# A spectral-mixing and expert kernel: all x of batch 0 loaded ahead of the weights, float64 conversions emitted behind the first FFT stage, GpSimd's tensor operations given to VectorE

## The chip, the core and the metric

The kernel runs on one core of a Trainium2 chip. The metric is device time in microseconds (us) from one launch. The engines are TensorE (PE; its weight loads are PEld), VectorE (DVE), ScalarE (ACT), GpSimd (POOL) and SyncE (SP), which here only issues DMAs. Each engine works through its own list of instructions in order, and waits on semaphores for the others.

## The reference

Three layers follow each other on x of 4 batches x 3072 positions x 256 channels.

```python
X = np.fft.fft(np.fft.fft(x, axis=1), axis=2).real          # 1: mixing by FFT
xp = concatenate([zeros, X[:, :-1]], axis=1)                # 2: channel mix with the position before
k = np.maximum((mu_k * X + (1 - mu_k) * xp) @ w_k, 0)       #    w_k 256 x 1024, w_r 256 x 256, w_v 1024 x 256: float64
y = sigmoid((mu_r * X + (1 - mu_r) * xp) @ w_r) * (k * k @ w_v)
e = argmax(y @ w_gate)                                      # 3: one of 8 experts for each token
out = softmax(y @ w_gate)[e] * sigmoid((y @ w_output_gate)[e]) * (relu(y @ w1[e]) @ w2[e])
```

## The kernel before

**Stage A, the FFT.** The 3072 positions are split into 24 x 128. In the first stage (`a_steps`, lines 264 to 290, called A1 here) seven x tiles of a batch, each of two windows of 512 columns (the last of one), are multiplied with a 120 x 120 matrix of cosines and sines (`fc`); ScalarE copies the products out of PSUM, and they are stored to a DRAM buffer, `scr`. An x tile is loaded by one DMA (`load_x`, line 243) whose pattern has 5 groups of 24 rows of 4 KB. For batch 0 the products overwrite the x tile, the matrices are float32 in one product, and GpSimd's queue issues the stores; for later batches x is split into a high and a low float32r half (ScalarE copies, another engine subtracts) and three products are added, and ScalarE's queue issues the stores. The second stage (A2, lines 291 to 375) reads `scr` back in six groups (`raw`, with tables `tb`), forms sum and difference `s` and `t` of the channel halves, folds them by symmetry (about eight short VectorE operations a group), and multiplies twice; the results go into `xt`, one batch in SBUF.

**Stage B, the channel mix.** `b_block` works on blocks of 512 tokens, six a batch, in the order `BLOCKS`. `mix_steps` forms the two mixed inputs and splits them into high and low halves. Eight steps f each take six matmuls with w_k, a relu and a square on ScalarE and VectorE with a split, and, two steps later, six matmuls with w_v. Between these steps `step(f)` advances A1 and A2 of the coming work and the mixing of the next block; `tail_steps` does the gate logits and writes rows and lists of tokens for stage C, the experts.

**The weights.** w_k, w_r and w_v come as float64 and are turned into two float32r halves by `convert` (line 195), nine units of 128 x 512: one DMA (`both`, 512 KB), on ScalarE an absolute value and a copy (the high half), on VectorE two integer operations (lines 213, 216) and three with two inputs (214, 215, 217), and on GpSimd two subtract-and-add operations for the low half (220, 221). Units 0 to 4 are w_r and w_k; they take buffers of the later `kh`, `kl`, `qh`, `ql` and `t1` tiles, and the fifth waits for the buffer of the first. Units 5 to 8 are w_v.

**GpSimd's tensor operations** are 34: two for each of nine conversions, `s` and `t` of four groups of batch 0 (lines 316, 317), and eight splits of x of batch 1 (line 281).

**What sets the order.** The program is written with a tile framework. Instructions are emitted by the Python code in the order in which it runs; a planner then walks through a modelled execution when the kernel is built, and at each moment gives each engine the first emitted of the instructions that are ready in its model. The result is one fixed list for each engine. SyncE issues nearly all loads. `load_later` keeps a load behind the second load of `raw` once that has been emitted. The start is emitted in the order of lines 531 to 541: seven x loads with the loads and conversions of w_r and w_k between them, constants, A1 of batch 0 (32 steps of its generator), the matrices `mc`, two groups of A2 (10 steps), small constants, the mixing of the first block, the clearing of the lists, and all four conversions of w_v. Block 0 follows.

Of the kernel before, what the change touches and what calls it, by code (L numbers as in the profile page):

```python
# [10 lines left out]
F32 = mybir.dt.float32  # L11
# [5 lines left out]
ALU = mybir.AluOpType  # L17
# [76 lines left out]
def moe_kernel(ctx: ExitStack, tc: tile.TileContext, x, mu_k, mu_r, wk2, wv2, wr2, wg, wo, w1, w2,  # L94
# [7 lines left out]
    def tt(o, a, b, op, eng=None):  # L102
        return (eng or DVE).tensor_tensor(out=o, in0=a, in1=b, op=op)  # L103
# [15 lines left out]
    a1 = sa.enter_context(tc.tile_pool(name="a1", bufs=2, side="right"))  # L119
    a2 = sa.enter_context(tc.tile_pool(name="a2", bufs=2, side="right"))  # L120

# [1 line left out]
    ident = const.tile([128, 128], F32, name="ident")  # L123
    acc = const.tile([128, 2, 5, E], BF16, name="acc")
    early = const.tile([128, 1, E], F32, name="early")
# [27 lines left out]
    def load_later(o, i):  # L153
        follow(SP.dma_start(o, i), raws[1:2], mybir.DependencyClass.NoSync, "the first groups come first")

    def split(h, l, src, eng=None):
        return act_copy(h, src), tt(l, src, h.bitcast(F32), ALU.subtract, eng)

    def setup_first():
        split(fh, fl, fc)  # L160
        POOL.memset(f0, 0.0)
        POOL.memset(xt[:, :, 0, 0:1], 0.0)
        POOL.memset(acc[:, 0, 0, :], 0.0)
        POOL.memset(early, 0.0)
        ACT.activation(out=ready, in_=early[:, 0], func=ACTF.Sigmoid)
        make_identity(nc, ident)
# [8 lines left out]
    def setup_second():  # L175
        mc = bp.tile([128, 2, 2, 128], F32, name="mc", tag="y", bufs=1)
        SP.dma_start(mc, c_m.rearrange("p (a b c) -> p a b c", a=2, b=2))
        split(mh, ml, mc)

    def setup_third():  # L180
        load_later(sm, c_s[:, 0:8 * E].rearrange("p (a b c) -> p a b c", a=2, b=4))
        load_later(cid, c_id.rearrange("p (a b c) -> p a b c", b=4, c=2))
        rt = bp.tile([128, 2, 128], F32, name="rt", tag="y", bufs=1)
        load_later(rt, c_r.rearrange("p (a b) -> p a b", a=2))
        act_copy(ones_tri, rt)
        wgf = bp.tile([128, 2, 2, E], F32, name="wgf", tag="lg", bufs=1)
        for j, m in enumerate((mu_k, mu_r)):
            load_later(mu[:, j], m.rearrange("(p c) -> p c", c=2))
        for j, w in enumerate((wg, wo)):
            load_later(wgf[:, :, j], w.rearrange("(c p) e -> p c e", p=128))  # L190
        DVE.tensor_scalar(omu, mu, -1.0, 1.0, ALU.mult, ALU.add)
        wgv = wgf.rearrange("p c j e -> p c (j e)")
        split(wgs[:, :, 0:16], wgs[:, :, 16:32], wgv)

    def convert(h, l, src):
        n = next(units)
        if n < 5:
            both = bp.tile([128, 1024], I32, name="both", tag="kh" if n % 2 else "kl")
            a = bp.tile([128, 512], I32, name="ca", tag="qh", bufs=3)
            b = bp.tile([128, 512], I32, name="cb", tag="ql", bufs=3)  # L200
            g = bp.tile([128, 512], F32, name="cg", tag="t1")
        else:
            if n == 5:
                spare.extend(bp.tile([128, 2, 512], d, name="spare", tag=t, bufs=1)
                             for d, t in ((I32, "yh"), (I32, "yl"), (F32, "y")))
            both = bp.tile([128, 1024], I32, name="both", tag="row")
            a, b, g = (t[:, n % 2] for t in spare)
        load_later(both.rearrange("p (a b) -> p a b", a=src.shape[1]), src.bitcast(I32))
        lo, hi = both[:, 0:1024:2], both[:, 1:1024:2]
        w = bp.tile([128, 512], F32, name="cw", tag="mx")  # L210
        af, bf = a.bitcast(F32), b.bitcast(F32)
        ACT.activation(out=g, in_=hi.bitcast(F32), func=ACTF.Abs)
        DVE.tensor_scalar(a, hi, 3, 0x3FFFFFF8, ALU.logical_shift_left, ALU.bitwise_and)
        stt(a, hi, -0x40000000, a, ALU.bitwise_and, ALU.bitwise_or)
        stt(af, g, SMALLEST, af, ALU.is_ge, ALU.mult)
        DVE.tensor_scalar(b, a, -0x800000, None, ALU.bitwise_and)
        stt(w, lo.bitcast(U32), 2.0 ** -52, bf, ALU.mult, ALU.mult)
        flat = lambda t: t.rearrange("p a b -> p (a b)")
        act_copy(flat(h), af)
        tt(af, af, flat(h).bitcast(F32), ALU.subtract, POOL)  # L220
        tt(flat(l), af, w, ALU.add, POOL)

    units, spare = iter(range(9)), []

    def convert_k(c, q):
        cols = slice(q * 512, q * 512 + 512)
# [7 lines left out]
        convert(wvh[:, 2 * q:2 * q + 2], wvl[:, 2 * q:2 * q + 2],  # L234
                wv2.rearrange("(c p) f -> p c f", p=128)[:, 2 * q:2 * q + 2])

# [1 line left out]
    def mm3(ps, ah, al, bh, bl, start=True, stop=True):  # L238
        PE.matmul(ps, ah, bh, start=start, stop=False)  # L239
        PE.matmul(ps, al, bh, start=False, stop=False)  # L240
# [8 lines left out]

    def load_first_x():  # L250
        places = [(a1, "xs", 3)] * 3 + [(bp, "yh", 1), (bp, "yl", 1), (bp, "rs", 1), (bp, "row", 2)]
        for i, (pool, tag, bufs) in enumerate(places):
            first_x.append(pool.tile([120, 2, 512], F32, tag=tag, name="xs", bufs=bufs))
            load_x(first_x[i], 0, i)
            if i == 0:
                SP.dma_start(fc, c_f)
            if i >= 3:
                early_units[i - 3]()
        early_units[4]()

    def a_steps(b):
        scr = dram.tile([24, 130, 256], F32, name="scr", tag="scr", bufs=2)
        sv = scr.rearrange("s (g m) d -> g s m d", g=5)
        for w in range(13):
            if w % 2 == 0:
                if b == 0:
                    e = xs = first_x[w // 2]
                else:
                    xs = a1.tile([120, 2, 512], F32, tag="xs", name="xs", bufs=3)
                    i = load_x(xs, b, w // 2)  # L270
                    follow(i, raws[2:3], mybir.DependencyClass.NoSync, "the first groups come first")
                    e = a1.tile([120, 2, 512], F32, tag="e", name="e", bufs=2)
            k_ = 120 if w < 12 else 96
            ps = pm.tile([120, 512], F32, tag="m", name="ps1")
            if b == 0:
                PE.matmul(ps[0:k_], fc[0:k_, 0:k_], xs[0:k_, w % 2], start=True, stop=True)
                yield
            else:
                h = a1.tile([120, 512], F32R, tag="xh", name="xh")
                l = a1.tile([120, 512], F32R, tag="xl", name="xl")  # L280
                split(h[0:k_], l[0:k_], xs[0:k_, w % 2], POOL if b == 1 and w < 8 else DVE)
                yield
                mm3(ps[0:k_], fh[0:k_, 0:k_], fl[0:k_, 0:k_], h[0:k_], l[0:k_])
            act_copy(e[0:k_, w % 2], ps[0:k_])
            if w % 2:
                (POOL if b == 0 else ACT).dma_start(sv[:, :, 2 * w - 2:2 * w + 2], e.rearrange("p w d -> p (w d)"))
                yield
            elif w == 12:
                (POOL if b == 0 else ACT).dma_start(sv[0:4, :, 24:26], e[0:96, 0])
            yield  # L290
# [18 lines left out]
        for i, ks in enumerate(GROUPS):  # L309
            load(i + 1)  # L310
            raw, tb = loaded.pop(i)
# [1 line left out]
            ns = raw.shape[1]  # L313
            s = a2.tile([128, ns, 128], F32, tag="s", name="s", bufs=1)
            t = a2.tile([128, ns, 128], F32, tag="t", name="t", bufs=1)
            tt(s, raw[:, :, 0:128], raw[:, :, 128:256], ALU.add, POOL if b == 0 and i >= 2 else DVE)
            tt(t, raw[:, :, 0:128], raw[:, :, 128:256], ALU.subtract, POOL if b == 0 and i >= 2 else DVE)
            special = ks[0] == 0
            f = f0 if special else a2.tile([128, nk, 2, 256], F32, tag="f2", name="f2")

# [53 lines left out]
                    act_copy(flat[:, top:top - nk * 128:-1], ps)  # L374
                yield

# [1 line left out]
    mixed = {}  # L378

    def mix_steps(j):  # L380
# [143 lines left out]
    def advance(b, n):  # L524
        if b < NB:
            if b not in gens:
                gens[b] = a_steps(b)
            for _ in range(n):
                next(gens[b], None)

    load_first_x()
    setup_first()
    advance(0, 32)
    setup_second()
    advance(0, 10)
    setup_third()
    for _ in mix_steps(BLOCKS[0]):
        pass
    clear_lists()
    for q in range(4):  # L540
        convert_v(q)

# [1 line left out]
    c1 = {}  # L544
    weights, xtile, meta, index, chunks, regs = {}, {}, {}, {}, {}, {}
    hq, outs, stores = {}, {}, []
# [227 lines left out]
    for n, (b, p) in enumerate(order):  # L774
        j = BLOCKS[p]
        mg = mix_steps(BLOCKS[order[n + 1][1]]) if n + 1 < len(order) else iter(())

        def step(f):
            ab_ = b if p <= 3 else b + 1
            if f <= 3:  # L780
                advance(ab_, 2 if f == 0 else 1)
            else:
                next(mg, None)
            if p <= 3:
                advance(b + 1, 1)
            if n == len(order) - 1:
                if f == 0:
                    early_plan()
                    for t in range(-EARLY, 0):
                        gather(t)  # L790
                split_w(-EARLY, f)
                if f == 7:
                    prep_x(-EARLY)

        vps, rs = b_block(b, j, step, tail)
        for _ in mg:
            pass
        for _ in tail:
            pass
        tail = tail_steps(n, vps, rs)  # L800
        if n == len(order) - 3:
            open_c1()
            load_w(-EARLY)
# [37 lines left out]
```

## Time and profile before

| | |
|---|---|
| timed runs | 1497.38, 1497.48, 1498.94 us (median 1497.48) |
| span of the profiled execution, first to last instruction | 1494.3 us |
| what lies around the span, against the median | 3.2 us |
| busy: PE, DVE, ACT, POOL | 1409.2, 1071.5, 947.5, 384.7 us |
| mean granted TensorE clock | 0.973 |

The profile is of one execution, whose own time is known by its span alone. Busy times are of an engine's own instructions; its waits and the issue of DMAs are not in them. A busy time by stages shows where an engine is full; the averages over the span hide that the first 115 us differ from the rest.

### The profile page before, as it was taken

The numbers are of one execution on the slowest core, as the hardware profiler recorded it, in microseconds if no ns is written. First come the engines' busy times: TensorE is split into PE (matmuls) and PEld (weight loads), VectorE is DVE, ScalarE is ACT, GpSimd is POOL, SyncE is SP. The second block draws the span as 40 slices with busy tenths as digits, with TensorE's granted clock in tenths as the row PEclk, the third lists the DMA queues.
The fourth block names the chain that finished last, engine by engine and source line by source line (L and its number), as shares of the span: only waits on it lengthen the run. The fifth ranks groups of instructions, "written<-read, shape, count | busy, mean of one in ns | idle before, by whom it ended". The sixth has DMA issues, their size and how long they took to land.

```text
span 1494.3 us, 25930 instructions
## 1 busy us (share of the span) xinstructions
PE 1409.2 (94%) x8973; PEld 1244.3 (83%) x8973; DVE 1071.5 (72%) x2235; ACT 947.5 (63%) x1952; POOL 384.7 (26%) x355
## 2 busy tenths in 40 slices
PE   4489989999989999899999999999999999999995
PEld 1367877888868888688888789999999999999995
DVE  1898667777767767677868657777777777777772
ACT  2466765677756676657658536666666666666662
POOL 2364111111111111111121233333433334433321
PEclk8699999999999999899999999999999999999998
DMA  6641232022231121220102112133111331232110
GB/s 197 200 139 62 75 102 81 30 68 79 82 99 55 49 68 53 82 67 27 37 16 72 52 37 92 54 100 101 55 48 44 101 94 42 64 110 70 45 33 19
DMA packets 63599, 108.33 MB, mean 72 GB/s; under 512 B 19209, under 2 KB 40849, under 8 KB 63461
## 3 DMA queue, kind: packets, MB, share of 16 engines
q1 hardware_dynamic: 45439, 68.28, 14.4%
q0 software_dynamic: 15472, 28.89, 6.5%
q10 hardware_dynamic: 2550, 9.44, 2.1%
q8 instruction: 72, 1.18, 0.4%
q14 instruction: 66, 0.54, 0.1%
HBM read 154.26 MB, written 39.88 MB: 130 GB/s over the span
## 4 chain that ended last, share of the span: by engine, by line
PE 84%; DMA 5%; DVE 4%; issue 4%; POOL 1%; ACT 1%; SPq 0%; POOLq 0%; DVEq 0%; ACTq 0%
PE hps L241 6%; PE hps L239 6%; PE hps L240 6%; PE o L662 6%; PE o L663 6%; PE o L664 6%; PE psk L239 6%; PE psk L241 6%; PE psk L240 6%; PE v L239 5%; PE v L241 5%; PE v L240 5%; PE ps L349 3%; PE ps L239 2%; DMA raw<-scr 1%
## 5 line engine op out<-in xcount | busy, mean ns | idle before, releaser
L469 POOL DMA_INDIRECT lists<-cid,pi x96 | 99.5, 1037 | 612.8 <-DVE pi L466 566.8
L106 DVE SCALAR_TENSOR_TENSOR hl<-hps,hh 128x512 fp32r<-128x512 f32 x204 | 140.9, 690 | 126.7 <-ACT hh L647 102.6
L647 ACT ACTIVATE hh<-hps 128x512 fp32r<-128x512 f32 x204 | 122.1, 598 | 168.4 <-PE hps L241 152.4
L587 POOL DMA_INDIRECT xg<-rows,ix x102 | 116.8, 1145 | 324.5 <-PE o L664 169.6
L106 DVE SCALAR_TENSOR_TENSOR t<-psk,t 128x512 f32<-128x512 f32 x192 | 132.3, 689 | 69.0 <-ACT t L507 67.7
L507 ACT ACTIVATE t<-psk 128x512 f32<-128x512 f32 x192 | 114.5, 596 | 87.9 <-PE psk L241 76.0
L103 DVE TENSOR_TENSOR ql<-t,qh 128x512 fp32r<-128x512 f32 x192 | 134.5, 701 | 43.4 <-ACT qh L100 41.5
L239 PE MATMUL psk<-kh,wkh 128*128 128x512 f32 x384 | 158.0, 412 | 0.7 <-DVE t L106 0.7
L241 PE MATMUL psk<-kl,wkh 128*128 128x512 f32 x384 | 152.6, 397 | 2.6 <-DVE kl L103 2.6
L241 PE MATMUL v<-ql,wvh 128*128 128x512 f32 x384 | 150.4, 392 | 2.9 <-DVE ql L103 2.9
L239 PE MATMUL v<-qh,wvh 128*128 128x512 f32 x384 | 152.7, 398 | 0.0
L100 ACT ACTIVATE qh<-t 128x512 fp32r<-128x512 f32 x192 | 120.6, 628 | 49.5 <-DVE t L106 47.1
L240 PE MATMUL psk<-kh,wkl 128*128 128x512 f32 x384 | 151.7, 395 | 0.0
L240 PE MATMUL v<-qh,wvl 128*128 128x512 f32 x384 | 149.9, 390 | 0.0
L103 DVE TENSOR_TENSOR wla<-raw,wha 128x512 fp32r<-128x512 f32 x200 | 130.8, 685 | 2.7
L103 DVE TENSOR_TENSOR wlb<-raw,whb 128x512 fp32r<-128x512 f32 x192 | 125.4, 685 | 2.6
L239 PE MATMUL hps<-xh,wha 128*128 128x256 f32 x432 | 123.4, 286 | 0.1
L670 POOL DMA_INDIRECT out<-o,ix x102 | 107.5, 1054 | 62.1 <-ACT o L669 32.6
L664 PE MATMUL o<-wla,hh 128*128 128x256 f32 x432 | 121.6, 282 | 0.6 <-issue 0.6
L662 PE MATMUL o<-wha,hh 128*128 128x256 f32 x432 | 122.0, 282 | 0.2 <-issue 0.2
L241 PE MATMUL hps<-xl,wha 128*128 128x256 f32 x432 | 121.9, 283 | 0.2
L663 PE MATMUL o<-wha,hl 128*128 128x256 f32 x432 | 121.9, 282 | 0.0
(193 smaller groups left out, 4115.5 us busy)
## 6 DMA issues: line engine op xcount, KB each, us to landing
raw<-in_moe_w SPq DMA_DIRECT2D x196, 512.0 KB
rows<-row SPq DMA_DIRECT2D x24, 530.0 KB
raw<-scr SPq DMA_DIRECT2D x24, 512.0 KB
xs<-in_x SPq DMA_DIRECT2D x24, 480.0 KB
scr<-e ACTq DMA_DIRECT2D x18, 480.0 KB
tb<-in_c_t SPq DMA_DIRECT2D x20, 256.0 KB
scr<-xs POOLq DMA_DIRECT2D x6, 480.0 KB
both<-in_moe_w_k SPq DMA_DIRECT2D x4, 512.0 KB
```

Source lines behind the costliest of these rows:

```text
L100: return ACT.activation(out=o, in_=i, func=ACTF.Copy, scale=scale)
L103: return (eng or DVE).tensor_tensor(out=o, in0=a, in1=b, op=op)
L106: return DVE.scalar_tensor_tensor(out=o, in0=a, scalar=s, in1=b, op0=op0, op1=op1, **kw)
L239: PE.matmul(ps, ah, bh, start=start, stop=False)
L240: PE.matmul(ps, al, bh, start=False, stop=False)
L241: return PE.matmul(ps, ah, bl, start=False, stop=stop)
L507: ACT.activation(out=t, in_=ps, func=ACTF.Relu)
L587: POOL.indirect_dma_start(xg[:, u], None, rows[0:nr], bass.IndirectOffsetOnAxis(ap=ix[:, u, 0:1], axis=0), bounds_check=nr - 1, oob_is_err ...
L647: marks[:] = [last, ACT.activation(out=h, in_=ps, func=ACTF.Relu), stt(l, ps, 0.0, h.bitcast(F32), ALU.max, ALU.subtract)]
L662: PE.matmul(ps, h[:, a, tok], wh[:, cols], start=f == 0, stop=False)
L663: PE.matmul(ps, l[:, a, tok], wh[:, cols], start=False, stop=False)
L664: PE.matmul(ps, h[:, a, tok], wl[:, cols], start=False, stop=f == 7)
```

## The change

All seven x tiles of batch 0 are loaded first, behind the small constant `fc`; the loads of four of the five w_r and w_k units are emitted behind them. `convert` is cut in two: it emits the load, and `convert_rest` emits the arithmetic of the oldest loaded unit. The arithmetic is emitted behind A1, spread over A2 and the mixing of the first block; the fifth unit's load is emitted behind the second arithmetic. The w_v units are loaded behind the clearing of the lists (two) and in steps 0 and 1 of block 0 (two), and their arithmetic is emitted in steps 0 to 3 of block 0. The loading of `mc` is emitted ahead of A1. GpSimd's 34 tensor operations are given to VectorE; GpSimd keeps memsets and DMAs. Comment lines that go are left out here.

```diff
@@ convert
         load_later(both.rearrange("p (a b) -> p a b", a=src.shape[1]), src.bitcast(I32))
+        loaded_w.append((h, l, both, a, b, g))
+
+    def convert_rest():
+        h, l, both, a, b, g = loaded_w.pop(0)
         lo, hi = both[:, 0:1024:2], both[:, 1:1024:2]
...
-        tt(af, af, flat(h).bitcast(F32), ALU.subtract, POOL)
-        tt(flat(l), af, w, ALU.add, POOL)
+        tt(af, af, flat(h).bitcast(F32), ALU.subtract)
+        tt(flat(l), af, w, ALU.add)
@@ load_first_x
+        SP.dma_start(fc, c_f)
         for i, (pool, tag, bufs) in enumerate(places):
             first_x.append(pool.tile([120, 2, 512], F32, tag=tag, name="xs", bufs=bufs))
             load_x(first_x[i], 0, i)
-            if i == 0:
-                SP.dma_start(fc, c_f)
-            if i >= 3:
-                early_units[i - 3]()
-        early_units[4]()
+        for unit in early_units[:4]:
+            unit()
@@ a_steps
-                split(h[0:k_], l[0:k_], xs[0:k_, w % 2], POOL if b == 1 and w < 8 else DVE)
+                split(h[0:k_], l[0:k_], xs[0:k_, w % 2])
...
-            tt(s, raw[:, :, 0:128], raw[:, :, 128:256], ALU.add, POOL if b == 0 and i >= 2 else DVE)
-            tt(t, raw[:, :, 0:128], raw[:, :, 128:256], ALU.subtract, POOL if b == 0 and i >= 2 else DVE)
+            tt(s, raw[:, :, 0:128], raw[:, :, 128:256], ALU.add)
+            tt(t, raw[:, :, 0:128], raw[:, :, 128:256], ALU.subtract)
@@ the start
     setup_first()
+    setup_second()
     advance(0, 32)
-    setup_second()
-    advance(0, 10)
+    convert_rest()
+    convert_rest()
+    early_units[4]()
+    advance(0, 1)
+    convert_rest()
+    advance(0, 4)
     setup_third()
+    convert_rest()
+    advance(0, 5)
     for _ in mix_steps(BLOCKS[0]):
         pass
+    convert_rest()
     clear_lists()
-    for q in range(4):
-        convert_v(q)
+    convert_v(0)
+    convert_v(1)
@@ step
+            if n == 0 and f < 4:
+                convert_rest()
+                if f < 2:
+                    convert_v(f + 2)
```

## Rows read from the trace of the kernel before

**Rows 1.** Busy time by stage: stretch, its length, busy us (instructions) by engine, clock, DMA
```profile
0.00:40.70 40.70, 20.67 (x24) 6.24 (x24) 9.26 (x15) 11.58 (x20) 10.99 (x19) 0.79 0.62 202
...
56.00:72.00 16.00, 11.31 (x64) 10.71 (x64) 12.33 (x35) 8.39 (x35) 4.09 (x3) 0.74 0.65 183
72.00:115.00 43.00, 35.03 (x143) 26.28 (x143) 42.97 (x56) 28.96 (x59) 25.75 (x15) 0.92 0.45 142
115.00:209.00 94.00, 93.97 (x472) 76.46 (x473) 72.77 (x152) 68.47 (x140) 18.57 (x15) 1.00 0.23 76
```
**Rows 2.** The chain that ended last, up to 115 us: start us, us, what
```profile
28.98 16.48 DMA both<-in_moe_w_k
...
66.28 5.55 DMA both<-in_moe_w_v
71.93 0.44 DVE spare L213
...
115.03 0.49 PE v L241
```
**Rows 3.** Timeline, first uses of x and weight tiles: start us, us, instruction [idle before <-releaser]
```profile
12.39 3.77 PE L276 MATMUL ps<-xs,fc 120*120 120x512 f32 x4 [0.76 <-DMA xs<-in_x]
...
17.16 1.95 PE L276 MATMUL ps<-xs,fc 120*120 120x512 f32 x4 [1.00 <-DMA xs<-in_x]
...
24.34 3.74 PE L276 MATMUL ps<-xs,fc 120*120 120x512 f32 x4 [5.23 <-DMA xs<-in_x]
...
25.77 0.43 DVE L213 TENSOR_SCALAR ca<-both 128x512 int32<-128x512 int32 x1 [17.37 <-DMA both<-in_moe_w_r]
...
30.75 3.74 PE L276 MATMUL ps<-xs,fc 120*120 120x512 f32 x4 [2.66 <-DMA xs<-in_x]
...
31.79 0.46 DVE L213 TENSOR_SCALAR ca<-both 128x512 int32<-128x512 int32 x1 [2.87 <-DMA both<-in_moe_w_k]
...
36.27 3.74 PE L276 MATMUL ps<-xs,fc 120*120 120x512 f32 x4 [1.79 <-DMA xs<-in_x]
...
37.75 1.42 DVE L213 TENSOR_SCALAR ca<-both 128x512 int32<-128x512 int32 x1 [2.79 <-DMA both<-in_moe_w_k]
...
43.06 1.23 PE L276 MATMUL ps<-xs,fc 96*96 96x512 f32 x2 [3.05 <-DMA xs<-in_x]
```
**Rows 4.** Timeline, from the last x tile to the first fold
```profile
44.33 0.59 ACT L100 ACTIVATE xs<-ps 96x512 f32<-96x512 f32 x1 [3.68 <-PE ps L276]
...
45.53 1.27 POOL L103 TENSOR_TENSOR ca<-ca,wkh 128x512 f32<-128x512 f32 x1 [3.92 <-ACT wkh L100]
...
46.75 0.71 POOL L289 DMA_DIRECT2D scr<-xs  x1
...
51.46 0.94 SPq L300 DMA_DIRECT2D raw<-scr  x2
...
56.13 0.68 DVE L103 TENSOR_TENSOR s<-raw 128x512 f32<-128x512 f32 x1
```
**Rows 5.** Timeline, VectorE and GpSimd side by side
```profile
81.97 1.71 POOL L103 TENSOR_TENSOR xl<-xs,xh 120x512 fp32r<-120x512 f32 x1
82.48 1.74 DVE L103 TENSOR_TENSOR kl<-mx,kh 128x512 fp32r<-128x512 f32 x1
83.64 1.73 POOL L103 TENSOR_TENSOR wvl<-spare,cw 128x512 fp32r<-128x512 f32 x1
```
**Rows 6.** Timeline, two VectorE operations behind each other with GpSimd idle
```profile
107.45 0.69 DVE L103 TENSOR_TENSOR rl<-mx,rh 128x512 fp32r<-128x512 f32 x1
...
108.06 0.69 DVE L103 TENSOR_TENSOR ql<-t,qh 128x512 fp32r<-128x512 f32 x1
```
**Rows 7.** VectorE from 56 to 115 us by form: group xcount | busy us, mean ns
```profile
L106 DVE SCALAR_TENSOR_TENSOR mx<-xt,omu,mx 128x512 f32<-128x512 f32 x8 | 7.5, 932 | 1.0 <-ACT mx L387 1.0
...
L103 DVE TENSOR_TENSOR s<-raw 128x512 f32<-128x512 f32 x2 | 1.4, 686 | 0.0
```
**Rows 8.** Timeline, the first fold of batch 1
```profile
224.38 0.69 DVE L103 TENSOR_TENSOR s<-raw 128x512 f32<-128x512 f32 x1 [6.93 <-DMA raw<-scr]
```

More of the change, by code (lines that the diff above doesn't have):

```diff
@@ L219, in convert @@
         act_copy(flat(h), af)
-        tt(af, af, flat(h).bitcast(F32), ALU.subtract, POOL)
-        tt(flat(l), af, w, ALU.add, POOL)
-    units, spare = iter(range(9)), []
+        tt(af, af, flat(h).bitcast(F32), ALU.subtract)
+        tt(flat(l), af, w, ALU.add)
+    units, spare, loaded_w = iter(range(9)), [], []
     def convert_k(c, q):
```

## The prediction

> **What bounds the kernel now.** I read the busy time by stage first [rows 1]. The reader is to see that TensorE is full from 115 us on (93.97 of 94 us) while VectorE has room there (72.77 of 94). Before 115 us it is the other way: from 72 to 115 us VectorE is busy 42.97 of 43 us and TensorE 35.03. So nothing in this change can be worth anything after 115 us, unless it disturbs the order of work; what counts is the moment at which TensorE becomes full. From there the rest of the kernel follows at TensorE's pace. The chain of waits says the same in order of time [rows 2]: up to 45 us it runs through loads of float64 weights, then over a load of w_v into VectorE at 71.93 us, and VectorE holds it until TensorE takes over at 115.03 us.
>
> Then I read how the x tiles and the weights arrive [rows 3]. The first use of an x tile comes 4.77 us after the one before it where nothing else is queued (12.39 to 17.16 us). A weight tile that is queued behind an x tile is first used 1.0 to 1.5 us after it (24.34 to 25.77, 30.75 to 31.79, 36.27 to 37.75 us), though it is larger (512 KB against 480 KB). So the x tiles are what the queue is slow at, and each weight ahead of x costs about as much as its small step. The last x tile is used at 43.06 us.
>
> Behind it stands a chain [rows 4]: the copy out of PSUM ends at 44.92 us, but the store to scr is issued by GpSimd at 46.75 us, because a GpSimd tensor operation of 1.27 us stands before it; the load of raw is issued at 51.46 us and the fold begins at 56.13 us.
>
> Last, the tensor operations on GpSimd and VectorE hold each other up [rows 5]. From 81.97 us they alternate: GpSimd 1.71, VectorE 1.74, GpSimd 1.73 us, one starting every 0.5 and 1.16 us in turn, so that a pair takes 1.67 us. Alone, such a VectorE operation takes 0.69 us and the next starts 0.61 us after it [rows 6].
>
> **The change part by part.** *x ahead of the weights.* Three weight tiles (w_r and two of w_k) stood before the last x tile; their steps are 1.43, 1.04 and 1.48 us [rows 3], together 3.95 us. The last x tile comes at 43.06 - 3.95 = 39.1 us. SyncE issues the same eight x and constant loads, only earlier; moving the small constant ahead of the first tile costs at most its own issue. The store of the last tile gains 46.75 - 44.92 = 1.83 us more, since GpSimd has nothing before it [rows 4]: issue at 41.0 us in place of 46.75. If its landing and raw's take as long as now (4.71 and 4.67 us), the fold could begin at 50.4 us. Four weight tiles now lie in the queue in front of raw, and each may cost a step of 1.0 to 1.5 us, 5.2 us in all; part of them is through by then. I take 52 us for the fold, with 50 and 55.5 us as bounds. The fifth weight's load waits on SyncE until the first conversion has given its buffer back, about 44 us; raw queues behind it, but is not ready before 45.7 us, so that wait is covered by 2 us.
>
> *The weights behind x.* This is the price. The first weight lands at about 39.1 + 1.3 = 40.4 us, not at 25.77. VectorE did the five conversions of w_r and w_k up to 56 us, in time in which it was idle anyway (9.26 us busy of the first 40.7) [rows 1]. Now it can begin at 40.4 us at the earliest.
>
> The Trainium skill (DMA: Bandwidth & Descriptors, section "Why a DMA increments its semaphore by 16 and not by 1") has a rule that speaks against the change here: a copy is spread over the largest number of engines, up to 16, that divides the slowest dimension on both sides. An x tile's pattern has 5 outermost, so by that rule it lies on 5 engines, and a weight tile on 16, of which these 5 serve all x first. The steps in rows 3 agree with it. By bytes alone, at the 202 GB/s of the first 40.7 us in rows 1, x and w_r (3.6 MB) would be through at 18 us, and the sum below would come out about 20 us lower at its start.
>
> *GpSimd's tensor operations on VectorE.* 34 of them: 18 in the conversions, 8 in the folds of batch 0, 8 in the splits of x of batch 1. What one adds to VectorE is 0.6 us; what it takes away is up to 1.05 us where VectorE was busy with an operation of two inputs (1.74 against 0.69), nothing where it was idle. After 115 us seven are left; they fall into VectorE's room, so they count nothing.
>
> *The sum.* VectorE's own work from 56 to 115 us [rows 1, 7]: 91 operations in 55.3 us. 49 of them are of 512 columns (rows 7: the first and the last of their 11 groups); at 0.60 us that is 29.4 us. Eight conversions of integers take 0.44 us by the row in the chain [rows 2], 3.5 us. Some 33 small ones make 8.6 us. That is 41.5 us of work where 55.3 were spent: 13.8 us was GpSimd's hold. To it come GpSimd's 18 operations of that stretch (3 and 15 in rows 1), 18 x 0.6 = 10.8 us, so this part alone gains 3 us. The five conversions of w_r and w_k come to VectorE's busy time: each 5 x 0.60 + 2 x 0.44 = 3.9 us, 19.4 us, and 0.6 us for the split of a constant. About four of the moved operations (two splits of x, one fold of a later group) needn't be done before block 0 ends: -2.4 us. Total 41.5 + 10.8 + 19.4 + 0.6 - 2.4 = 69.9 us. From 40.4 us on this ends at 110.3 us if VectorE never waits. It was idle 3.7 us between 56 and 115 us [rows 1] (59 less 55.3); conversions with nothing beside them are a chain through ScalarE, and I put 3 us. So 113.3 us in place of 115.0: 1.7 us less.
>
> Bounds. Idle time may be 0 to 7 us (the upper end is VectorE waiting for raw with one conversion done, below). The first weight may land at 40.4 us or as late as 44 us, the fourth weight's time now. Both at their ends give 110 to 121 us, so -5 to +6 us. That TensorE starts block 0 sooner is no gain of its own while VectorE is late; with the w_v conversions now placed between the steps of block 0, VectorE has 3.9 us more in each of four steps where TensorE has about 2.8, and the room after f = 3 takes it back.
>
> The sum is made against the profiled execution, whose span is 1494.3 us; the median of the timed runs is 1497.48 us, 3.2 us more, and I take that as unchanged. Forecast: 1497.5 - 1.5 = **1496.0 us**, a little less than the 1.7 because TensorE has a few filler matmuls fewer to do meanwhile.
>
> **The rivals.** *Faster: VectorE stops being the bound.* From 56 to 115 us TensorE is idle 59 - 11.31 - 35.03 = 12.7 us [rows 1]. If the conversions are done mostly between 40 and 52 us and the hold is worth more than I count, the start of the folds decides (4 us earlier) and half of TensorE's 8 us of idle time between 72 and 115 us goes too: 8 us, 1489.5 us. For it speaks how clean the alternation in rows 5 is; against it that the 19.4 us of conversions have only 12 us before the fold.
>
> *Slower: VectorE stands at the fold.* The order on VectorE is laid down by a planner when the kernel is built, and it can be out of step with the loads: at the first fold of batch 1 VectorE stands 6.93 us for raw [rows 8]. If here it puts the fold of raw behind one conversion only, VectorE does that one alone from 40.4 to about 44.9 us, then stands until raw is there at 52 us, with w_k already loaded: 7 us lost, and everything behind it, from the conversions to block 0, ends at 120 us. That gives 1497.5 + 5 = 1502.5 us. It decides once the wait for raw exceeds the 3 us of idle time in my sum. For it: the conversions were covered by waits for x until now, and are in competition with the fold from now on. Against it: the first two conversions are emitted ahead of the fold and have precedence.
>
> *No effect:* the planner sends the loads in much the same order, or the stores to scr take up what the weights leave. Then only the 3 us of GpSimd's hold less some disturbance is left, within 2 us of 1497.5.
>
> **How the numbers follow.** Forecast 0.50 (its own range 1492 to 1500), VectorE no longer the bound 0.25, VectorE standing at the fold 0.20, no effect 0.05. About 0.2% (3 us) is what a measurement of this kernel can tell from no change. Of the forecast's half, 0.12 lies below 1494.5 us, 0.33 within 3 us of before and 0.05 above; with the rivals that makes faster 0.37, same 0.36, slower 0.27. The range takes most of both rivals: 1487 to 1504 us.
>
> **What would show it.** Right: the last x tile used near 39 us, the first weight near 40.5, the fold near 52; no tensor operation on GpSimd, VectorE operations of 512 columns at 0.69 us throughout; VectorE full from 41 to about 113 us, and TensorE full from there. Wrong: a weight used well before the last x tile (then the loads aren't bound as rows 3 say), VectorE idle for over 5 us between 41 and 113 us (then the order counts), or TensorE full well before VectorE's backlog ends (then VectorE was not the bound). A wait that grows at a later batch's first fold would be outside this sum altogether.

## The result and the profile after

The kernel after takes **1504.51 us** (median; 1503.75 to 1506.71 us) against 1497.43 us of the kernel before (four runs of each): 7.1 us more, ratio 1.0056 [1.0043, 1.0069] (a 95% interval, as in all that follows). The forecast was 1496.0 us. The profiled execution has a span of 1502.0 us (before 1494.3) and a mean granted clock of 0.969 (0.973). It took 1503.75 us, so 1.75 us lie around its span; the 3.2 us that the prediction added set the span of one execution against the median of others.

Busy time by stage of the kernel after, in the stretches and columns of [rows 1], with the stretch from 40.7 to 56 us added:

```profile
0.00:40.70 40.70, 18.11 (x24) 5.64 (x24) 0.56 (x2) 6.57 (x11) 4.97 (x14) 0.79 0.56 174
40.70:56.00 15.30, 2.02 (x2) 0.39 (x2) 11.84 (x22) 7.88 (x14) 2.02 (x3) 0.50 0.61 180
56.00:72.00 16.00, 7.27 (x36) 6.72 (x36) 9.44 (x26) 4.94 (x21) 0.00 (x0) 0.61 0.61 175
72.00:115.00 43.00, 33.93 (x156) 26.89 (x157) 38.70 (x77) 27.79 (x61) 0.00 (x0) 0.92 0.47 149
115.00:209.00 94.00, 93.14 (x465) 75.13 (x464) 77.98 (x170) 70.15 (x147) 11.79 (x8) 1.00 0.26 80
```

VectorE is full in none of the first four stretches: 59.98 us of the 74.3 between 40.7 and 115 us. TensorE loses 4.0 us against before from 56 to 72 us (7.27 for 11.31), 1.1 from 72 to 115 us and 0.8 behind that. So neither engine is the bound at the start. What is, the timeline from 28 us on shows:

```profile
29.14 3.74 PE L278 MATMUL ps<-xs,fc 120*120 120x512 f32 x4 [4.23 <-DMA xs<-in_x]
...
35.40 3.74 PE L278 MATMUL ps<-xs,fc 120*120 120x512 f32 x4 [2.52 <-DMA xs<-in_x]
...
41.25 0.43 DVE L217 TENSOR_SCALAR ca<-both 128x512 int32<-128x512 int32 x1 [38.07 <-DMA both<-in_moe_w_r]
41.25 0.67 ACT L216 ACTIVATE cg<-both 128x512 f32<-128x512 f32 x1 [15.70 <-DMA both<-in_moe_w_r]
...
41.82 1.07 ACT L100 ACTIVATE xs<-ps 120x512 f32<-120x512 f32 x2
...
42.45 2.02 PE L278 MATMUL ps<-xs,fc 96*96 96x512 f32 x2 [3.31 <-ACT xs L100]
...
43.18 0.71 POOL L288 DMA_DIRECT2D scr<-xs  x1 [16.72 <-ACT xs L100]
...
45.39 0.33 SPq L154 DMA_DIRECT2D both<-in_moe_w_k  x1
45.70 0.63 POOL L288 DMA_DIRECT2D scr<-xs  x1 [1.81 <-ACT xs L100]
...
46.32 0.69 POOL L291 DMA_DIRECT2D scr<-xs  x1
```

Read the ScalarE rows first. From 25.55 us it does nothing for 15.70 us, and what ends the wait is the load of a weight, w_r, for the absolute value of the first conversion (line 216). Products of two x tiles have been lying in PSUM since about 33 and 39 us (29.14 + 3.74 and 35.40 + 3.74). Their copies stand behind that one instruction in ScalarE's list and start at 41.82 us. GpSimd waits 16.72 us for the copies, TensorE 3.31 us for PSUM (the pool has four buffers, and these two tiles fill four), and the last three stores to `scr` are issued between 43.18 and 46.32 us, in one bunch and in the middle of the weights. SyncE's list is fixed too: it stands for the fifth weight's buffer until 45.39 us, and two loads of tables (`tb`, 384 and 256 KB) go out only behind that load, from 45.76 us on.

The chain of waits goes on from there (start us, us, what; the longest pieces):

```profile
14.03 29.20 DMA both<-in_moe_w_k
45.70 0.62 POOL scr L288
46.32 12.18 DMA scr<-xs
58.58 3.87 DMA raw<-scr
62.48 0.69 DVE s L103
```

The last store lands 12.18 us after its issue, where it took 4.71 us before. The row of the timeline that answers to the last one of [rows 4], with two rows of the third conversion around it, and the first folds of batches 1 to 3, which answer to [rows 8]:

```profile
51.44 0.63 ACT L100 ACTIVATE wkh<-ca 128x512 fp32r<-128x512 f32 x1 [3.17 <-DVE ca L106]
...
62.48 0.69 DVE L103 TENSOR_TENSOR s<-raw 128x512 f32<-128x512 f32 x1 [9.20 <-DMA raw<-scr]
...
65.42 0.68 DVE L103 TENSOR_TENSOR ca<-ca,wkh 128x512 f32<-128x512 f32 x1
...
229.80 0.69 DVE L103 TENSOR_TENSOR s<-raw 128x512 f32<-128x512 f32 x1 [7.15 <-DMA raw<-scr]
...
434.21 0.69 DVE L103 TENSOR_TENSOR s<-raw 128x512 f32<-128x512 f32 x1 [8.16 <-DMA raw<-scr]
...
637.98 0.69 DVE L103 TENSOR_TENSOR s<-raw 128x512 f32<-128x512 f32 x1 [7.32 <-DMA raw<-scr]
```

and the later two in the kernel before:

```profile
427.59 0.69 DVE L103 TENSOR_TENSOR s<-raw 128x512 f32<-128x512 f32 x1 [7.03 <-DMA raw<-scr]
...
630.07 0.69 DVE L103 TENSOR_TENSOR s<-raw 128x512 f32<-128x512 f32 x1 [7.19 <-DMA raw<-scr]
```

VectorE stands 9.20 us at the fold although it has work: the third conversion's `wkh` was ready at 52.07 us, but the operation that uses it is behind the fold in VectorE's list and runs at 65.42 us.

The first fold is 6.35 us late (62.48 for 56.13), the first fold of batch 1 is 5.42 us late, that of batch 2 6.62, that of batch 3 7.91, and the span ends 7.7 us late. About 5.4 us are made before the first fold of batch 1 and 2.3 behind it. Of these, 1.1 and 0.1 us stand in the longer waits at the first folds of batches 2 and 3; where the rest arises isn't shown.

### The profile page after: what moved, and what is told of

It reads as the page before. It is cut to its first block, busy times and chain, and to the rows that moved or that the text cites. A ratio compares the mean times of both kernels' runs of the same rounds, so it can differ in the third digit from the quotient of the medians.

```text
span 1502.0 us, 25905 instructions
## 1 busy us (share of the span) xinstructions
PE 1408.4 (94%) x8973; PEld 1244.3 (83%) x8973; DVE 1065.1 (71%) x2269; ACT 950.0 (63%) x1952; POOL 343.3 (23%) x321
## 4 chain that ended last, share of the span: by engine, by line
PE 86%; DMA 6%; issue 3%; DVE 2%; ACT 1%; SPq 1%; POOL 1%; POOLq 0%; ACTq 0%
PE hps L243 6%; PE hps L245 6%; PE hps L244 6%; PE psk L243 6%; PE o L673 6%; PE o L672 6%; PE o L674 6%; PE psk L245 6%; PE psk L244 6%; PE v L243 6%; PE v L244 6%; PE v L245 5%; PE ps L351 4%; DMA both<-in_moe_w_k 2%; DMA raw<-scr 2%
## 5 line engine op out<-in xcount | busy, mean ns | idle before, releaser
L471 POOL DMA_INDIRECT lists<-cid,pi x96 | 103.0, 1073 | 710.6 <-DVE pi L468 670.0
L597 POOL DMA_INDIRECT xg<-rows,ix x102 | 121.5, 1191 | 315.0 <-PE hps L245 178.9
L244 PE MATMUL hps<-xh,wla 128*128 128x256 f32 x432 | 121.8, 282 | 0.0
```

The lines of the kernel that those rows point to most:

```text
L597: POOL.indirect_dma_start(xg[:, u], None, rows[0:nr], bass.IndirectOffsetOnAxis(ap=ix[:, u, 0:1], axis=0), bounds_check=nr - 1, oob_is_err ...
```

## The experiments

Theory at this point: ScalarE's list, with `cg<-both` ahead of the copies, makes the stores, and with them `raw` and the fold, late. Rivals: the GpSimd operations given to VectorE; the weights that come late in themselves; the fifth weight's load in front of `raw`.

**Copies first.** The kernel after, and the conversions' absolute value is held behind the thirteenth copy in ScalarE's list, without a semaphore. The loads keep their order, except that the fifth weight's load now follows the first load of `raw`, because the buffer that it waits for comes free later, and that the tables, no longer behind it, go out from 29.22 us on.

```diff
-            act_copy(e[0:k_, w % 2], ps[0:k_])
+            copies.append(act_copy(e[0:k_, w % 2], ps[0:k_]))
...
-        ACT.activation(out=g, in_=hi.bitcast(F32), func=ACTF.Abs)
+        i = ACT.activation(out=g, in_=hi.bitcast(F32), func=ACTF.Abs)
+        follow(i, copies[12:13], mybir.DependencyClass.NoSync, "the copies of the first stage come first")
```

> The changed kernel, with ScalarE's part of the first conversions ordered behind ScalarE's last copy of batch 0's first FFT stage; the order of loads stays as in the changed kernel. Theory A (ScalarE's list: the absolute value of w_r, which lands at 41.2 us, stands ahead of the copies of the fifth to seventh x tile): the stores of tiles five, six and seven are issued near 34, 40 and 42 us instead of 43.2, 45.7 and 46.3, the first fold starts at 51 to 55 us instead of 62.5, and the kernel takes 1493 to 1498 us. Theory B (the loads: x, weights and stores share DMA engines, and whatever is put ahead of raw delays it by its size): the stores land no earlier than 56 us whenever they are issued, the fold starts at 60 us or later, and the kernel stays within 2 us of 1504.5.

Measured: 1497.59 us, ratio 1.0005 [0.9996, 1.0015]: the loss is gone. The timeline of this kernel:

```profile
39.17 1.99 PE L279 MATMUL ps<-xs,fc 96*96 96x512 f32 x2 [0.95 <-DMA xs<-in_x]
...
41.95 0.67 ACT L216 ACTIVATE cg<-both 128x512 f32<-128x512 f32 x1 [0.16 <-DMA both<-in_moe_w_r]
42.09 0.69 POOL L292 DMA_DIRECT2D scr<-xs  x1 [2.32 <-ACT xs L100]
...
50.60 0.39 SPq L303 DMA_DIRECT2D raw<-scr  x1
...
54.65 0.69 DVE L103 TENSOR_TENSOR s<-raw 128x512 f32<-128x512 f32 x1 [1.47 <-DMA raw<-scr]
```

ScalarE waits 0.16 us for the same load, and the weight lands no earlier (41.95 us). The stores of the fifth to seventh tile go out at 34.01, 39.15 and 42.09 us, as expected, and the fold comes 7.8 us earlier than in the kernel after.

**The fifth weight alone.** This run takes apart the two things that moved there: the kernel after with its own ScalarE order, and the fifth load emitted behind two loads of `raw`.

```diff
     convert_rest()
-    early_units[4]()
     advance(0, 1)
+    early_units[4]()
     convert_rest()
```

> The changed kernel with only the load of the fifth w_r/w_k unit moved behind the first two loads of raw, as it came to stand in the run with ScalarE's copies first; ScalarE's list stays that of the changed kernel. It is the control for that run. If ScalarE's list is the cause, this keeps the late stores (43, 46, 46 us) and stays at 1502 to 1506 us. If the fifth weight's share of the DMA engines was the cause, the first fold starts below 57 us and it falls to 1496 to 1499 us.

Measured: 1501.96 us, ratio 1.0043 [1.0026, 1.0060]. The time is just below the 1502 to 1506 us that were expected if ScalarE's list is the cause, and the fold above the 57 us expected if it is the fifth weight: both have a part. ScalarE still waits, and the fold comes halfway:

```profile
42.03 0.68 ACT L216 ACTIVATE cg<-both 128x512 f32<-128x512 f32 x1 [15.18 <-DMA both<-in_moe_w_r]
...
46.79 0.69 POOL L291 DMA_DIRECT2D scr<-xs  x1
...
54.74 0.95 SPq L302 DMA_DIRECT2D raw<-scr  x2
58.56 0.69 DVE L103 TENSOR_TENSOR s<-raw 128x512 f32<-128x512 f32 x1 [4.73 <-DMA raw<-scr]
```

The three stores go out as late and as close together as in the kernel after (43.97, 46.17 and 46.79 us), yet the last lands 7.8 us after its issue and not 12.18, so the bunch isn't what made that landing so long. With the copies first, where there is no bunch, it is 8.4 us. More than the one load moved: the two loads of tables that stood behind it on SyncE go out from 29.44 us on and not from 45.76.

The fold's 7.8 us split into 3.9 for the fifth load and the tables behind it, which no run parts (62.48 to 58.56), and 3.9 for ScalarE's order (58.56 to 54.65). In time the order is worth 0.38% (1.0043 to 1.0005, with intervals that don't meet), 5.7 us. The fifth load's 0.13%, 1.9 us, isn't told from nothing by the times, as its interval overlaps that of the kernel after; it is shown in the trace alone.

**GpSimd's operations, alone and taken back.** The kernel before with its 34 operations on VectorE, and the kernel after with them on GpSimd:

```diff
-        tt(af, af, flat(h).bitcast(F32), ALU.subtract, POOL)
-        tt(flat(l), af, w, ALU.add, POOL)
+        tt(af, af, flat(h).bitcast(F32), ALU.subtract)
+        tt(flat(l), af, w, ALU.add)
...
```

> The kernel before with GpSimd's 34 tensor operations given to VectorE and nothing else changed. By the prediction's sum this part alone takes 3 us off VectorE between 56 and 115 us, and the last store is issued 1.8 us earlier: 1492 to 1496 us. If the hold between the two engines were not what filled VectorE, the 18 operations would add 10.8 us to a full engine: 1503 us or more.

Measured: 1496.28 us, ratio 0.9996 [0.9987, 1.0006]: nothing that can be told. Its row of busy time from 72 to 115 us:

```profile
72.00:115.00 43.00, 35.74 (x145) 27.97 (x146) 37.37 (x71) 27.74 (x55) 0.00 (x0) 0.88 0.33 106
```

VectorE now has 5.6 us to spare there, and TensorE has gained 0.7 us only. The chain of waits of that kernel says what came in its place:

```profile
63.59 10.15 DMA xs<-in_x
73.76 0.63 ACT xh L100
74.39 0.53 ACT rh L100
...
80.30 4.94 DMA both<-in_moe_w_v
85.26 0.43 DVE spare L213
```

An x tile of batch 1 arrives at 73.74 us, and the copy `rh` that the next matmuls want stands behind its split on ScalarE: VectorE stands 2.00 us for `rh` and TensorE 4.29. The chain then runs over a load of w_v, but VectorE has other work meanwhile and stands only 0.28 us for it; 2.08 more are a wait for ScalarE at 99.46 us. So part of the room that the edit makes goes to a wait for x; that all of it goes to loads isn't shown.

> The changed kernel with the 34 tensor operations back on GpSimd; the new order of loads and conversions stays. If the order is the whole loss and GpSimd's part is a gain, this is slower than the changed kernel by the gain of that part, 2 to 5 us: 1506 to 1510 us. If VectorE's extra operations are the loss, this is back at 1498 to 1501 us.

Measured: 1508.16 us, ratio 1.0075 [1.0058, 1.0092], 0.19% above the kernel after, with intervals that overlap. In the trace GpSimd's hold is there again: a GpSimd operation runs from 84.37 to 85.65 us, and one of VectorE that starts at 84.49 us takes 1.72 us instead of 0.68.

```profile
84.37 1.28 POOL L103 TENSOR_TENSOR spare<-spare,wvh 128x512 f32<-128x512 f32 x1 [1.62 <-ACT kh L100]
84.49 1.72 DVE L103 TENSOR_TENSOR kl<-mx,kh 128x512 fp32r<-128x512 f32 x1
```

Its first fold comes at 61.14 us, 1.3 us before that of the kernel after, and its first fold of batch 1 at 233.75, 4.0 us after. So in the new order this part looks like a gain of about 3 us, which the rest of the change more than eats; the times alone don't tell it from nothing.

**The loads between x again.** The kernel after with all it has, but w_r and w_k loaded between the last x tiles as before:

```diff
             load_x(first_x[i], 0, i)
-        for unit in early_units[:4]:
-            unit()
+            if i >= 3:
+                early_units[i - 3]()
```

> The changed kernel with the loads of w_r and w_k back between the last x tiles (the constant still first); the arithmetic of the conversions still emitted behind the first FFT stage, all tensor operations on VectorE. Theory A and B both say that the order of loads is what hurts: w_r is used near 26 us again, the first fold starts at 53 to 57 us, and the kernel takes 1491 to 1497 us. If the later place of the arithmetic in the program is the loss, the loads change little and it stays above 1501 us.

Measured: 1494.65 us, ratio 0.9986 [0.9976, 0.9995]: 9.9 us less than the kernel after and a little less than before. In its trace w_r is used at 26.55 us, the last x tile at 45.20 us, 6.0 us later than with the copies first, and the first fold at 56.68 us after a wait of 2.79 us, only 2.0 us later. So "all x ahead of the weights" is the harmful edit, and the others, without it, gain about 2 us. This kernel is also 2.9 us faster than the one with the copies first (0.9986 against 1.0005, the intervals just don't meet), although its fold comes later. So ScalarE's order isn't all that the weights behind x cost. VectorE has worked 8.29 us by 40.7 us here and 0.56 there, which speaks for the price that the prediction named, conversions that begin late; no run shows that alone.

**The x tile's pattern.** All of these orders share the slow x tile. Next I put the 24 rows outermost and the 5 groups inside, with the rows and columns of the matrix `fc` permuted to match, in the loads and in the stores; the last tile carries an unused fifth group, which in batch 3, where it would read past the end of x, is loaded in four pieces.

```diff
-    f = np.zeros((5, 24, 5, 24))
+    f = np.zeros((24, 5, 24, 5))
...
-                f[g, :, g, q] = part
+                f[:, g, q, g] = part
...
-        src = bass.AP(x.tensor, x.offset + (b * S + 4 * i) * D, [(26 * D, ng), (128 * D, 24), (1, nm * D)])
+            src = bass.AP(x.tensor, x.offset + (b * S + 4 * i + 128 * r0) * D, [(128 * D, nr), (26 * D, ng), (1, nm * D)])
...
-        sv = scr.rearrange("s (g m) d -> g s m d", g=5)
+        sv = scr.rearrange("s (g m) d -> (s g) m d", g=5)
```

> The kernel before with another layout of the first stage's tiles: the 24 rows outermost and the 5 groups inside, on the x side and on the store side (the matrix's rows and columns are permuted to match; the last tile carries the unused fifth group along). By the steps between first uses, an x tile's load is slow because of its outer 5. Then an x tile takes about 2 us of the queue in place of 4.7, the last x tile is used at 25 to 33 us instead of 43, the first fold starts 8 to 15 us earlier, the stalls at the first folds of later batches (7 us each) shrink by 2 to 4 us, and the kernel takes 1475 to 1488 us. If the x loads are slow for another reason (4 KB rows, rows far apart), nothing changes: 1495 to 1499 us.

Measured, on the kernel before: 1465.13 us, ratio 0.9788 [0.9772, 0.9804], 32 us less, more than the 9 to 22 us that were expected. Its busy time in the first stretch, its first uses of the third and the fourth x tile, which have no weight between them, and its first folds of batch 0 and batch 1:

```profile
0.00:40.70 40.70, 16.42 (x26) 5.17 (x26) 18.25 (x27) 15.57 (x27) 16.17 (x25) 0.84 0.80 255
...
13.16 1.95 PE L285 MATMUL ps<-xs,fc 120*120 120x512 f32 x4 [0.84 <-DMA xs<-in_x]
...
15.87 1.95 PE L285 MATMUL ps<-xs,fc 120*120 120x512 f32 x4 [0.76 <-DMA xs<-in_x]
...
43.85 0.68 DVE L103 TENSOR_TENSOR s<-raw 128x512 f32<-128x512 f32 x1
...
209.23 0.69 DVE L103 TENSOR_TENSOR s<-raw 128x512 f32<-128x512 f32 x1 [3.19 <-DMA raw<-scr]
```

The same 480 KB arrive 2.71 us apart, not 4.77 as the second and third tile of the kernel before, or 7.18 as its third and fourth (17.16 to 24.34) [rows 3]; the first fold comes 12.3 us earlier, and the wait at the border falls from 6.93 us [rows 8] to 3.19.

With the loads alone in this order, and the stores in the old one:

```diff
-    f = np.zeros((5, 24, 5, 24))
+    f = np.zeros((24, 5, 5, 24))
...
-                f[g, :, g, q] = part
+                f[:, g, g, q] = part
```

> The kernel before with the 24 rows outermost on the x side alone; the stores keep 5 outermost (this is the half of the layout that the loads have). If the x loads carry the gain, the last x tile is used below 34 us and most of the 32 us is here: 1465 to 1476 us. If the stores carry it, the fold waits for them as before and the kernel takes 1485 us or more.

Measured: 1480.30 us, ratio 0.9886 [0.9871, 0.9902], between the two ranges that were expected. The first fold comes at 43.67 us, as early as with both, and the border waits as long as before:

```profile
213.20 0.69 DVE L103 TENSOR_TENSOR s<-raw 128x512 f32<-128x512 f32 x1 [7.14 <-DMA raw<-scr]
```

So the loads carry 17 us and the stores 15 us. The trace shows 11.2 us of the loads' part by the first fold of batch 1 (213.20 for 224.38). The stores' part comes at the borders: 4.0, 7.2 and 12.0 us by the first folds of batches 1, 2 and 3, whose waits are 4.0, 2.7 and 6.1 us shorter with the stores in this order too.

The other edits on this layout need no diff of their own. The kernel after:

> The changed kernel with the same layout. ScalarE's list keeps the absolute value of w_r ahead of the copies of the last tiles, but w_r now lands when its x tiles do, before 25 us, so the wait of 15.7 us in front of these copies falls under 4 us. If the cause is this wait, the loss against the kernel before with the same layout vanishes: both within 4 us of each other, 1474 to 1488 us. If the loss is something that the order of the arithmetic carries with it, this stays 5 us or more above it.

Measured: 1465.51 us, ratio 0.9782 [0.9760, 0.9804], the same as the kernel before in this layout. ScalarE's wait for w_r is 5.20 us there (w_r is used at 22.02 us), a little above the 4 us expected but not 15.70, and no loss can be told any more. The kernel with the copies first, run twice:

> The same layout on the changed kernel with ScalarE's copies first. If the wait is gone already by the layout, this differs from the changed kernel in that layout by less than 3 us.

> The version with ScalarE's copies first and the whole layout, once more beside the other two on one chip: 1462 to 1466 us, and not told apart from them unless one differs by over 2 us.

Measured: 1463.41 us, ratio 0.9782 [0.9766, 0.9799], and 1465.47 us, ratio 0.9784 [0.9771, 0.9797]. So ScalarE's order is worth nothing that can be told once x comes fast. GpSimd's operations on VectorE in the kernel before:

> The kernel before with the tensor operations on VectorE and the whole layout. In the old layout waits for x of batch 1 and for w_v took the place of GpSimd's hold; in the new one x of batch 1 lands sooner, so the 3 us of the sum should show: 1460 to 1464 us against 1465.1 with GpSimd kept. If it stays at 1465, VectorE is not what bounds this stretch in either layout.

Measured: 1463.57 us, ratio 0.9774 [0.9759, 0.9789], no more than 1.6 us from the same without that edit. And the loads between x:

> The changed kernel with the weights' loads back between the last x tiles, and the whole layout. With quick x tiles the place of the weights is worth little: within 3 us of 1464 us. If the weights still cost their step ahead of the last x tile, it is 3 us or more slower than the version with ScalarE's copies first.

Measured: **1456.48 us**, ratio 0.9731 [0.9716, 0.9746], the best of all, 41 us below the kernel before. The expectation (within 3 us of 1464) was missed: it is 7.5 us below. Busy time by stage, first of this kernel, then of the kernel after in this layout, which differs from it in the place of the weights' loads alone:

```profile
0.00:40.70 40.70, 17.11 (x26) 5.61 (x26) 17.06 (x32) 14.86 (x28) 6.15 (x17) 0.75 0.81 273
40.70:56.00 15.30, 11.64 (x64) 10.94 (x64) 12.90 (x38) 9.23 (x37) 0.00 (x0) 0.78 0.78 213
56.00:72.00 16.00, 13.41 (x59) 10.21 (x60) 14.04 (x28) 11.53 (x22) 0.00 (x0) 0.89 0.70 200
```

```profile
0.00:40.70 40.70, 16.09 (x28) 6.28 (x29) 14.50 (x31) 15.42 (x32) 6.05 (x17) 0.77 0.83 278
40.70:56.00 15.30, 11.24 (x64) 10.27 (x62) 13.65 (x36) 8.63 (x28) 0.00 (x0) 0.83 0.77 238
56.00:72.00 16.00, 13.39 (x46) 9.87 (x47) 13.55 (x27) 10.00 (x21) 0.00 (x0) 0.79 0.52 147
```

The intervals of the two ratios don't meet (0.9746 and 0.9760 are their nearest ends), so the place of the loads is the cause. TensorE has done 123 matmuls from 40.7 to 72 us against 110, and the first fold of batch 1 comes at 199.61 us against 202.12. That is 2.5 of the 8.5 us between the two spans (1455.3 and 1463.8). The first fold of batch 0 is no earlier (39.83 against 38.59 us), but w_r is used at 16.38 us and not at 22.02, and VectorE has worked 17.06 us of the first 40.7 and not 14.50. That the conversions begin sooner is thus the likely way; it was not tried, and where the other 6.0 us arise stays open.

## Why the prediction was wrong

- **The last x tile at 39.1 us**: right as a sum of loads. With ScalarE out of the way it is used at 39.17 us. In the kernel after it is used at 42.45 us, because PSUM was full. The model behind it, that each weight ahead of x costs its small step, was only right in the sum: without weights between them the last full tiles still come 6.3 to 6.6 us apart (22.55, 29.14, 35.40 us). [rows 3] had shown as much: 7.18 us lie between 17.16 and 24.34 us, with no weight between the two tiles. That the sum came out is in part luck.
- **The last store issued at 41.0 us, the fold at 52 us, between 50 and 55.5 us: this is the step that failed.** They came at 46.32 and 62.48 us. I had the last tile's chain start at its load, and asked of GpSimd's queue alone what stood in front of the store. I did not ask it of ScalarE, where the planner had put the first conversion's absolute value ahead of the copies of three x tiles. Loading the weight behind x turned that harmless place into a wait of 15.70 us. That is 5.3 us of the miss. The larger part is the landing, which I had left at 4.71 us and which took 12.18. It is 4.5 to 4.7 us in the three kernels with weights between the x tiles (the kernel before, the same with GpSimd's operations on VectorE, and the loads between x again), 7.8 and 8.4 us with four weights behind x (the fifth weight alone, the copies first), and 12.18 us with the fifth weight and the tables behind x too. With the copies first the store is issued at 42.09 us, the fold at 54.65 lies inside the bounds, and the kernel takes 1497.59 us.
- **"That wait is covered by 2 us"**, of the fifth weight in front of `raw`: wrong in the trace. Its load, issued at 45.39 us, lies among the stores, and not only `raw` stood behind it on SyncE but also two loads of tables, which the prediction did not have. Together they move the fold by 3.9 us.
- **The first weight at 40.4 us**: right, 41.25 us. The slow x tiles do hold what is behind them: with quick ones w_r is used at 22.02 us. Where the prediction was silent is that this pattern, and not the order, was the lever: 32 us.
- **GpSimd's operations gain 3 us**: the hold is gone (VectorE's operations of 512 columns take 0.69 us), and in the new order the size is near (0.19%, not told from nothing by the times). In the old order it is nothing (0.9996): VectorE gets its 5.6 us of room, and TensorE 0.7 us of work out of it.
- **The sum, 69.9 us of VectorE from 40.4 us with 3 us idle**: VectorE was not the bound. It is idle 14.3 us between 40.7 and 115 us, 9.20 of them at the fold. This was the sign that I had named for an order that counts (over 5 us idle).
- **The rivals.** "VectorE stands at the fold", 1502.5 us with a chance of 0.20, is what happened in effect, at 1504.5 us. Its mechanism is there in part: the planner did put the fold ahead of conversion work that was ready, and VectorE stood with w_k loaded. But VectorE had work until 53.28 us, so by these rows the fold's place would have cost nothing with the fold's data there at 52 us, as I had it; it was `raw` coming 10 us later that made it cost. No run moved the fold alone, so the shares of the two stay open.
- **Outside the sum**, as the prediction said of a wait that grows at a later batch's first fold: 2.5 of the 7.9 us by the first fold of batch 3, of which 1.3 us are longer waits for `raw` there.

The Trainium skill (DMA: Bandwidth & Descriptors, section "Why a DMA increments its semaphore by 16 and not by 1") says that the largest number up to 16 that divides the slowest dimension of both sides is the number of engines a copy runs on. By it the x load goes from 5 to 12 (24 rows in memory, 120 partitions). By the rule alone I estimate a step of 4.77 x 5 / 12 = 2.0 us; the trace has 2.71, so it agrees in direction and not wholly in size, and no run here shows the engines one by one. It was cited in the prediction as a price of the change; it should have been read as what limits the start.

## What to carry to other kernels

When a load is moved back, look up every instruction that consumes it, on every engine, and ask what stands behind that instruction in the engine's list: a consumer that was harmless while its data came early holds up all that follows. Here the planner's list had such a consumer ahead of work that was ready; why it was put there isn't shown. Freeing an engine that looks full is worth what the next wait leaves, so find that wait first. And where transfers of the same size arrive at different speeds, repair the slow one's pattern before reordering: here the orders of loading moved the time by up to 10 us, and the pattern by 32.

## What the runs showed of the hardware

- The order of the dimensions alone changes the step of a load of 480 KB from 4.77 us, or 7.18 between the same two tiles, to 2.71 us, and in the first 40.7 us the rate from 202 GB/s [rows 1] to 255 GB/s (the kernel before in that layout).
- The last tile's store of 192 KB landed 4.71 us after its issue in the kernel before, 8.4 us after it with four weights loaded behind x, and 12.18 us with the fifth weight and the tables there too. Two other stores just ahead of it were no hindrance that shows (7.8 us).
- Taking GpSimd off VectorE's way shortens an operation from 1.72 or 1.74 to 0.69 us, and still moved the time of the kernel before by nothing (0.9996).
